# A chunked-attention and feed-forward kernel: a second seven-product scheme, also for part of the first layer, and a small addition moved to GpSimd

## The chip, the cores and the metric

The kernel runs on one core of one Trainium2 chip. The metric is device microseconds (us) of one execution; the time of the kernel before is the median of three runs. A profiled execution gives, beside its own time, a trace of every instruction, whose times count from the first instruction of the span. Engines are named PE (TensorE matmul), PEld (its weight load), DVE (VectorE), ACT (ScalarE), POOL (GpSimd) and SP (SyncE).

## The reference

```python
# q, k, v: (8, 8, 576, 64), chunks of 64 rows
scores = 0.125 * q_c @ k_c^T                  # within a chunk, 64 x 64
attn = exp(scores - max) / (sum + 1e-9)       # along the last axis
x = (attn @ v_c)                              # as 4608 tokens x 512 (heads side by side)
h = x @ w_in                                  # 512 -> 2048
g = maximum(0.01 * h, h)
out = g @ w_out                               # 2048 -> 512, float32
```

## The kernel before, in words

**Tiling.** 4608 tokens are 36 units of 128 tokens (two chunks of 64 rows each). Attention is done unit by unit; its result goes, transposed and in fp16, into a ring xT of 1536 tokens. The feed-forward part goes by blocks of tokens (`BLOCKS`, line 178): four of 128, four of 256, six of 512.

**One unit of attention.** q and k come by DMA issued from POOL (fp32 in DRAM, fp16 in SBUF), are transposed on PE (units 0 to 8, q also 13 and 18) or by a DMA of SP, q is spread into a zeroed tile QZ by two copies (POOL for the later units, line 240), PE makes the scores Sp (line 494), DVE takes the maximum and subtracts it (503, 509), ACT exponentiates (535), DVE sums (542), adds 1e-9 (544), takes the reciprocal (546) and multiplies (552); the result is transposed on PE (tpe, units 0 to 8 and 19) or by SP, PE multiplies with v (xp, line 586), and ACT writes the ring (597).

**First layer.** For each block, units "A" of PE: 512 columns of PSUM, made of 8 matmuls of 256 columns (16 of 128 in the four small blocks), line 679; ACT evacuates each with the leaky function into gT (line 693).

**Second layer.** The four small blocks are multiplied plainly (oP, line 704). In the others the block's tokens, the 2048 inner columns and the 512 output columns are each halved, and the 2x2 by 2x2 product is made of seven products ("M", line 776), each 8 matmuls of 256 columns for every 128 rows. Five of the seven take a sum of two quarters of gT, made by DVE ("form", line 753), and five a sum of quarters of w_out (WF, line 731, made once). Products 3, 2 and 1 open a PSUM bank each (ma, mb, mc), and others add to the same bank once its earlier content has been read; DVE and ACT put the results together (lines 806 to 816) and SP stores them.

**What sets the order.** `Planner` (line 22) holds all tasks with an engine, assumed durations, dependencies and a position, walks through a model of time, and emits each instruction at its planned turn; every engine and queue then runs its instructions strictly in that order. The names that steer it: `LEAD`, `ATT` (how far attention runs ahead of the blocks), `A_LEAD` (by how much of a block the first layer ends before the second layer of the block before), `MARGIN`, `HOLD`, `TWEAK`. Where PE would have a gap before 24 us, `fill` (line 942) puts idle matmuls in. PSUM has six banks for all products of this kind ("mm").

Of the kernel before, what the change touches and what calls it, by code (L numbers as in the profile page):

```python
# [21 lines left out]
class Planner:  # L22
# [61 lines left out]
    def run(self):  # L84
# [8 lines left out]
        while self.can or self.landings or any(self.queues.values()):  # L93
# [55 lines left out]
def kernel(  # L149
# [22 lines left out]
    NIN = 9  # L172
    G = 2 * CH
# [6 lines left out]
    SUBS = {}  # L180
    LEAD = 3.59
# [5 lines left out]
    ATT = -0.46  # L187
# [4 lines left out]
    EXP8 = ()  # L192
    EARLY_V = 0
    HOLD = {('v', 3): 28.7, ('vb', 1, 1): 15.3, ('k', 2): 14.1, ('q', 5, 0): 31.9, ('G', 0, 2, 0): 20.9, ('vb', 0, 0): 3.7, ('cast', 'q'): 5.0, ('n', 0): 11.9, ('k', 3): 18.8, ('c', 0): 15.1, ('e', 0): 13.3, ('tq', 4): 24.6, ('G', 0, 3, 0): 28.9, ('s', 2): 15.0, ('G', 2, 2, 0): 32.7, ('q', 5, 1): 29.5}
    EARLY_Q = ("SP",)
    T_EXP8 = 0.2
    FILL = 24.0
    FILLS = 0.8
    MARGIN = 0.6
    TWEAK = {(4, 12): 0.39, (5, 5): -0.14, (0, 4): -0.39, (17, 1): -0.17, (5, 4): -0.05, (17, 5): -0.31, (32, 1): 0.26, (33, 5): -0.04, (34, 0): 0.31}  # L200
    A_LEAD = 0.23
# [12 lines left out]
    VS = sbp.tile([128, H // 2, max(EARLY_V, 2), 128], FP16, name="VS")  # L214
# [4 lines left out]
    WF = sbp.tile([128, 5, HB, HM], FP16, name="WF")  # L219
# [10 lines left out]
    copy = {"DVE": (0.40, 0.46), "ACT": (0.52, 0.62), "POOL": (0.61, 0.66)}  # L230
# [96 lines left out]
    vf = sbp.tile([128, H // 2, max(EARLY_V, 2), D], FP32, name="v_f")  # L327

    def load_early(c, m):
        def emit(eng, tag, at):  # L330
            part = slice(m * CH, (m + 1) * CH)
            (nc.sync if eng == "SP" else nc.scalar).dma_start(
                out=vf[part, :, c, :],
                in_=v[0, m * H // 2:(m + 1) * H // 2, c * CH:(c + 1) * CH, :].rearrange("h j d -> j h d"),
            )
        return emit

    def cast_early(c, m):
        def emit(eng, tag, at):
            part = slice(m * CH, (m + 1) * CH)  # L340
            either(eng, VS[part, :, c:c + 2, part], vf[part, :, c:c + 2, :])
        return emit
# [6 lines left out]
    for c in range(EARLY_V):  # L349
        for m in range(2):  # L350
            add(("early", c, m), {e: (0.42, 0.42) for e in EARLY_Q}, load_early(c, m), [("land_f", "q0")], pos=-25 + c + 0.1 * m,
                dma=("first", 0.23, 1 / 1120))
    for c in range(0, EARLY_V, 2):
        for m in range(2):
            add(("zs", c, m), {"DVE": (0.1 + 0.105 * EARLY_V, 0.13 + 0.105 * EARLY_V)}, zero_early(m), [("warm",)], pos=-28) if c == 0 else None
            add(("vs", c, m), {"DVE": (0.46, 0.48), "ACT": (0.53, 0.62)}, cast_early(c, m),
                [("early", c, m), ("early", c + 1, m)], pos=-9.5 + c / 2)
            for e in range(2):
                v_parts.setdefault(c + e, []).extend([("vs", c, m), ("zs", 0, m)])

    def add_load(what):
# [6 lines left out]
        elif kind == "v":  # L368
# [4 lines left out]
            if b >= NVB:  # L373
                users = [u for u in range(NU) for e in range(2)
                         if (2 * u + e) // NCH == b - NVB]
                deps += [("v", max(users))]
            load(("v", b, m, c0), load_v(b, m, c0, c1), deps, (c1 - c0) * 256, "row")
            for c in range(c0, c1):
                if b * NCH + c >= EARLY_V:
                    v_parts.setdefault(b * NCH + c, []).append(("landed", "v", b, m, c0))  # L380
        elif kind == "Q":
# [27 lines left out]
    def zero_vb(i, m):  # L409
        def emit(eng, tag, at):  # L410
            to = empty(i, m)
            if eng == "DVE":
                nc.vector.memset(to, 0.0)
                return
            for t in range(2):
                part = to[:, 2 * t:2 * t + 2]
                nc.scalar.activation(
                    out=part, in_=zeros[m * CH:(m + 1) * CH, 0:1].unsqueeze(2).unsqueeze(3).to_broadcast(part.shape),
                    func=AFT.Copy, bias=0.0, scale=1.0,
                )  # L420
# [13 lines left out]
    for i in range(NVB):  # L434
        for m in range(2):
            add(("vb", i, m), {"ACT": (2.1, 2.2)} if (i, m) == (0, 0) else {"DVE": (1.02, 1.05)} if i == 0 else {"DVE": (1.02, 1.05), "ACT": (2.1, 2.2)}, zero_vb(i, m), [("warm",)] if i == 0 else [("n", 0)], pos=-27 if i == 0 else -6.0)
# [36 lines left out]
    def copy_k(u):  # L473
        def emit(eng, tag, at):
            st["KT", u] = sbp.tile([128, 4, 2, CH], FP16, name="KT", tag="KT", bufs=6)
# [3 lines left out]
    def turn_dma(name, u):  # L479
        def emit(eng, tag, at):  # L480
            n = {"q": "QT", "k": "KT"}[name]
            st[n, u] = sbp.tile([128, 4, 2, CH], FP16, name=n, tag=n, bufs={"q": 4, "k": 6}[name])
# [32 lines left out]
    def negative(u):  # L515
        def emit(eng, tag, at):
            st["nm", u] = sbp.tile([128, 8], FP32, name="nm", tag="nm", bufs=2)
            nc.vector.tensor_scalar_mul(out=st["nm", u], in0=st["mx", u], scalar1=-SCL)
        return emit

    def expo8(u):
        def emit(eng, tag, at):
            st["ex", u] = sbp.tile([128, 8, CH], FP16, name="ex", tag="ex", bufs=2)
            st["z", u] = sbp.tile([128, 8], FP32, name="z", tag="z", bufs=2)
            for i in range(8):
                nc.scalar.activation(
                    out=st["ex", u][:, i, :], in_=st["S", u][:, i, :], func=AFT.Exp,
                    bias=st["nm", u][:, i:i + 1], scale=SCL, accum_out=st["z", u][:, i:i + 1],
                )
        return emit  # L530

# [6 lines left out]
    def total(u):  # L538
        def emit(eng, tag, at):
            if u not in EXP8:  # L540
                st["z", u] = sbp.tile([128, 8], FP32, name="z", tag="z", bufs=2)
                nc.vector.tensor_reduce(out=st["z", u], in_=st["ex", u], axis=AXL.X, op=ALU.add)  # L542
            ze = sbp.tile([128, 8], FP32, name="ze", tag="ze", bufs=2)
            nc.vector.tensor_scalar_add(out=ze, in0=st["z", u], scalar1=1e-9)
            st["zi", u] = sbp.tile([128, 8], FP32, name="zi", tag="zi", bufs=2)
            nc.vector.reciprocal(out=st["zi", u], in_=ze)
        return emit

    def norm(u):
        def emit(eng, tag, at):  # L550
            st["en", u] = sbp.tile([128, 8, CH], FP16, name="en", tag="en", bufs=3)
# [13 lines left out]
    def copy_e(u):  # L565
        def emit(eng, tag, at):
            st["et", u] = sbp.tile([128, 2, 2, 2, CH], FP16, name="et", tag="et", bufs=4)
# [3 lines left out]
    def turn_e_dma(u):  # L571
        def emit(eng, tag, at):
            st["et", u] = sbp.tile([128, 2, 2, 2, CH], FP16, name="et", tag="et", bufs=4)
# [26 lines left out]
    def units1(j):  # L600
        n = BLOCKS[j] // sub(j)
        return [(j, a, h) for h in range(n) for a in range(NFC * sub(j) // 512)]

    def tile_units(u):
# [3 lines left out]
        return [("A",) + x for x in units1(j) if x[2] == h]  # L608

    for u in range(NU):  # L610
        p = att
        for n, name in enumerate("qk"):
# [6 lines left out]
            else:  # L619
                before = [x for x in range(u) if x not in BY_PE["q"]] if name == "q" else list(range(u))  # L620
                deep = {"q": 4, "k": 6}[name]
# [4 lines left out]
        if u in BY_PE["k"]:  # L626
            add(("k", u), {e: copy[e] for e in ("DVE", "ACT")}, copy_k(u), [("tk", u)] + ([("s", u - 6)] if u >= 6 else []), pos=p(u, 3))
        qdep = [("tq", u)]
        for s in range(2):
            add(("q", u, s), qe, spread_q(u, s), qdep + [("s", u - 3) if u >= 3 else ("qz", u)], pos=p(u, 2 + s))  # L630
        kt = ("k", u) if u in BY_PE["k"] else ("tk", u)
        add(("s", u), {"PE": (0.233, 0.40)}, scores(u), [("q", u, 0), ("q", u, 1), kt], pos=p(u, 4), bank="Sp", frees=[("x" if u in EXP8 else "b", u)])
# [3 lines left out]
        if u in EXP8:  # L636
            add(("nm", u), {"DVE": (0.17, 0.2)}, negative(u), [("m", u)] + freed, pos=p(u, 6))
            add(("x", u), {"ACT": (8 * T_EXP8, 8 * T_EXP8 + 0.1)}, expo8(u), [("nm", u), ("exp",)] + prev, pos=p(u, 7))
        else:
            add(("b", u), dve, shift(u), [("m", u)] + freed, pos=p(u, 6))  # L640
            add(("x", u), {"ACT": (0.53, 0.64)}, expo(u), [("b", u), ("exp",)] + prev, pos=p(u, 7))
        tz = 0.41 if u in EXP8 else 1.11
        add(("z", u), {"DVE": (tz, tz + 0.03)}, total(u), [("x", u)] + prev, pos=p(u, 8))
        ne = {"DVE": (0.70, 0.74), "POOL": (1.2, 1.25)}
        add(("n", u), {e: ne[e] for e in (NORM if u >= 9 else ("DVE",))}, norm(u),
            [("z", u)] + ([("e", u - 3)] if u >= 3 else []), pos=p(u, 9))
        ready = ("n", u)
        if u in BY_PE["e"]:
            add(("e", u), {"PE": (0.223, 0.39)}, turn_e(u), [ready, ("ident",)], pos=p(u, 10), bank="ox", frees=[("c", u)])
            add(("c", u), {e: copy[e] for e in ("DVE", "ACT")}, copy_e(u), [("e", u)] + ([("v", u - 4)] if u >= 4 else []), pos=p(u, 11))  # L650
        else:
            add(("e", u), {"SP": (1.3, 1.3)}, turn_e_dma(u), [ready] + ([("v", u - 4)] if u >= 4 else []), dma=("turn", 0.9, 0.0014), pos=p(u, -5))
        vd = [("c", u) if u in BY_PE["e"] else ("e", u)]
        for e in range(2):
            vd += v_parts[2 * u + e]
            if 2 * u + e >= EARLY_V:
                vd += [("vb", (2 * u + e) // NCH % NVB, m) for m in range(2)]
# [9 lines left out]
    def gT(j):  # L667
        return GT[START[j] // 512][:, :, START[j] % 512:START[j] % 512 + BLOCKS[j]]

# [16 lines left out]
    def act1(j, a, h):  # L686
        def emit(eng, tag, at):
            tb = sub(j)
            nf = 512 // tb
            n = START[j] // 512  # L690
            if n not in GT:
# [291 lines left out]
```

## Time and profile before

| | |
|---|---|
| median of three runs | 285.53 us (284.9 to 286.17) |
| the profiled execution, its own time | 285.76 us |
| its span, first to last instruction | 284.0 us |
| granted TensorE clock | 1.000 |
| PE busy | 273.4 us, 96% of the span |
| DVE, ACT, POOL busy | 200.6, 158.3, 130.4 us |

Rows of groups read: line, engine, operation, output and inputs, shape, count, then busy time and the mean of one in ns, then the idle time of the engine just before them and what ended it. Matmuls overlap in the pipeline (a row's mean is longer than the distance between two), so PE's pace is read from the chain of waits, where a stretch of so many matmuls has a length. Rows of the timeline begin with the start and the length in us, and end in brackets with the idle time before and what ended it.

### The profile page before, as it was taken

What the parts mean: (1) busy time and instruction counts of PE and PEld (TensorE: products, weight loads), DVE (VectorE), ACT (ScalarE), POOL (GpSimd) and SP (SyncE); (2) the same over time, 40 slices, a digit from 0 to 9 for tenths busy, and PEclk for the clock granted to TensorE, in tenths of its full rate; (3) what the DMA queues carried; (4) which work ended last, traced back from release to release, by engine and by line L of the source; (5) the groups of instructions that cost most, each with busy time, mean ns of one, the idle gap of its engine ahead of it and who ended that gap; (6) DMA issues with size and microseconds to landing.
All of it is one profiled execution on the core that took longest, in us unless ns stands there. A gap on an engine that the chain in (4) does not pass through costs nothing.

```text
span 284.0 us, 7425 instructions
## 1 busy us (share of the span) xinstructions
PE 273.4 (96%) x3076; PEld 241.2 (85%) x3076; DVE 200.6 (71%) x357; ACT 158.3 (56%) x282; POOL 130.4 (46%) x162
## 2 busy tenths in 40 slices
PE   6789999999999999999999999999999999999995
PEld 5689956778889899999899999999999999888884
DVE  6677848969897869779767987595759671810472
ACT  6279825774557476676566456545565564345320
POOL 8848655767964916645845693682230000000000
PEclk9999999999999999999999999999999999999999
DMA  8999999999999999999999999999924110400043
GB/s 142 154 190 169 176 180 155 215 134 174 146 167 174 176 161 133 185 146 158 178 130 161 151 144 196 154 128 196 155 58 166 21 32 9 150 0 2 0 168 130
DMA packets 164194, 38.77 MB, mean 137 GB/s; under 512 B 155200, under 2 KB 159808, under 8 KB 164160
## 3 DMA queue, kind: packets, MB, share of 16 engines
q0 software_dynamic: 114336, 18.09, 94.9%
q1 hardware_dynamic: 48784, 19.93, 42.1%
q8 instruction: 24, 0.39, 0.6%
q10 hardware_dynamic: 1040, 0.26, 0.5%
q14 instruction: 10, 0.08, 0.2%
HBM read 36.70 MB, written 9.44 MB: 162 GB/s over the span
## 4 chain that ended last, share of the span: by engine, by line
PE 81%; DMA 9%; POOL 7%; ACT 1%; issue 1%; DVE 0%; POOLq 0%
PE hT L679 39%; PE mb L776 13%; DMA k_in<-in_k_dram 9%; PE mc L776 9%; PE ma L776 9%; PE oP L704 4%; PE xp L586 3%; PE Sp L494 3%; POOL QZ L240 2%; POOL q_in L277 2%; POOL VB L285 1%; POOL k_in L277 1%; POOL w_inT L294 1%; ACT gT L693 1%; PE tpe L561 0%
## 5 line engine op out<-in xcount | busy, mean ns | idle before, releaser
L679 PE MATMUL hT<-xT,w_inT 128*128 128x256 f16 (+1 forms) x1280 | 141.8, 262 | 0.1
L693 ACT ACTIVATE gT<-hT 128x512 f16<-128x512 f32 x144 | 85.1, 597 | 69.8 <-PE hT L679 65.9
L679 PEld LDWEIGHTS <-w_inT 128*128 128x128 f16 x1280 | 113.3, 98 | 11.8 <-issue 0.3
L240 POOL COPY QZ<-QT 64x512 f16<-64x512 f16 x50 | 39.0, 780 | 34.9 <-DMA QT<-q_in 20.7
L776 PEld LDWEIGHTS <-gT 128*128 128x128 f16 x512 | 49.2, 98 | 5.5
L753 DVE TENSOR_TENSOR S<-gT 128x2048 f16<-128x2048 f16 (+1 forms) x30 | 30.8, 1055 | 15.8 <-ACT gT L693 15.8
L776 PEld LDWEIGHTS <-S 128*128 128x128 f16 x384 | 36.6, 98 | 4.2 <-issue 0.2
L277 POOL DMA_DIRECT2D q_in<-in_q_dram x39 | 33.2, 853 | 11.1 <-DMA q_in<-in_q_dram 5.4
L277 POOL DMA_DIRECT2D k_in<-in_k_dram x39 | 33.1, 849 | 10.4 <-DMA k_in<-in_k_dram 3.4
L542 DVE TENSOR_REDUCE z<-ex 128x8 f32<-128x512 f16 x36 | 24.5, 680 | 16.3 <-ACT ex L535 16.1
L776 PE MATMUL mb<-WF,gT 128*128 128x256 f16 x256 | 33.2, 273 | 0.0
L503 DVE TENSOR_REDUCE mx<-Sp 128x8 f32<-128x512 f32 x36 | 24.2, 672 | 7.6 <-PE Sp L494 7.5
L285 POOL DMA_DIRECT2D VB<-in_v_dram x16 | 18.5, 1159 | 21.5 <-PE xp L586 15.4
L597 ACT ACTIVATE xT<-xp 128x512 f16<-128x512 f32 x36 | 21.3, 593 | 10.3 <-PE xp L586 10.2
L552 DVE TENSOR_TENSOR en<-ex,zi 128x512 f16<-128x512 f16 x36 | 25.1, 697 | 0.4
L509 DVE TENSOR_TENSOR sh<-Sp,mx 128x512 f32<-128x512 f32 x36 | 24.6, 684 | 0.4
L535 ACT ACTIVATE ex<-sh 128x512 f16<-128x512 f32 x36 | 22.5, 626 | 3.3 <-DVE sh L509 2.8
L753 DVE TENSOR_TENSOR gT<-gT 128x2048 f16<-128x2048 f16 (+1 forms) x20 | 20.3, 1025 | 0.0
L236 ACT ACTIVATE QZ<-qp 64x512 f16<-64x512 f16 x14 | 8.2, 589 | 15.4 <-PE qp L462 9.6
L776 PE MATMUL ma<-w_outT,S 128*128 128x256 f16 x128 | 16.6, 273 | 0.1
L776 PE MATMUL mc<-WF,S 128*128 128x256 f16 x128 | 16.6, 273 | 0.0
L776 PE MATMUL ma<-WF,gT 128*128 128x256 f16 x128 | 16.6, 273 | 0.0
(53 smaller groups left out, 251.4 us busy)
## 6 DMA issues: line engine op xcount, KB each, us to landing
out_dram<-osb SPq DMA_DIRECT2D x10, 512.0 KB, 3.7
VB<-in_v_dram POOLq DMA_DIRECT2D x16, 288.0 KB, 10.6
q_in<-in_q_dram POOLq DMA_DIRECT2D x31, 128.0 KB, 11.5
k_in<-in_k_dram POOLq DMA_DIRECT2D x31, 128.0 KB, 10.7
out_dram<-osb SPq DMA_DIRECT2D x14, 256.0 KB, 6.8
w_inT<-in_moe_w_in_dram POOLq DMA_DIRECT2D x8, 256.0 KB, 7.7
w_outT<-in_moe_w_out_dram POOLq DMA_DIRECT2D x4, 512.0 KB, 11.1
q_in<-in_q_dram POOLq DMA_DIRECT2D x8, 64.0 KB, 11.6
```

The costliest lines, as they stand in the source:

```text
L240: nc.gpsimd.tensor_copy(out=out, in_=in_)
L277: nc.gpsimd.dma_start(out=qk[name, u][a - u * G:z - u * G], in_=SRC[name][a // S, :, a % S:a % S + z - a, :].rearrange("h p d -> p h d"),)
L285: nc.gpsimd.dma_start(out=VB[b % NVB][m * CH:(m + 1) * CH, :, c0:c1, m * CH:(m + 1) * CH], in_=v[b, m * H // 2:(m + 1) * H // 2, c0 * CH:c ...
L503: nc.vector.tensor_reduce(out=st["mx", u], in_=st["S", u], axis=AXL.X, op=ALU.max)
L509: nc.vector.tensor_tensor(out=st["sh", u], in0=st["S", u], in1=st["mx", u].unsqueeze(2).to_broadcast((128, 8, CH)), op=ALU.subtract,)
L535: nc.scalar.activation(out=st["ex", u], in_=st["sh", u], func=AFT.Exp, bias=0.0, scale=SCL)
L542: nc.vector.tensor_reduce(out=st["z", u], in_=st["ex", u], axis=AXL.X, op=ALU.add)
L552: (nc.vector if eng == "DVE" else nc.gpsimd).tensor_tensor(out=st["en", u], in0=st["ex", u], in1=st["zi", u].unsqueeze(2).to_broadcast((12 ...
L679: nc.tensor.matmul(out=hT[:, i, :], lhsT=w_inT[:, t, fc * 128:(fc + 1) * 128], rhs=xT[:, t, r0 % RING:r0 % RING + tb], start=(t == 0), sto ...
L693: nc.scalar.activation(out=gT(j)[:, nf * a:nf * a + nf, h * tb:h * tb + tb], in_=HT.pop((j, a, h)), func=AFT.Prelu, bias=0.0, scale=1.0, a ...
L753: nc.vector.tensor_tensor(out=to, in0=of, in1=by, op=op)
L776: nc.tensor.matmul(out=to, lhsT=lhs[:, fc, p * 128:(p + 1) * 128], rhs=rhs[:, fc, :], start=(opens and (p == 0 or j == LAST) and fc == 0), ...
```

## The change

**Second layer.** The seven products are now these (A is gT, B is w_out, both in quarters): 1 = A11 B11, 2 = A12 B21, 4 = A22 T4, 5 = S5 B12', 6 = S6 T2, 7 = S7 T3, 3 = S3 B22. There are four sums of gT instead of five, two of them made from an earlier one, and four of w_out instead of five, one written over B12 itself. ACT reads out products 1 and 2, DVE five sums as before. The products' order is 1, 6, 5, 7, 2, 4, 3; product 2 adds to the bank of 1, products 7 and 4 to that of 6, product 3 to that of 5. A product waits only for the quarters of gT that it reads.

```diff
+        (WF[:, 0], B22, B12, ALU.subtract), (WF[:, 1], WF[:, 0], B11, ALU.add), (WF[:, 2], B21, WF[:, 1], ALU.subtract),
+        (B12, B12, B11, ALU.subtract),
...
+                5: lambda: (a21, a22, ALU.add, None), 6: lambda: (SF[j, 5], a11, ALU.subtract, None),
+                7: lambda: (a11, a21, ALU.subtract, a21), 3: lambda: (a12, SF[j, 6], ALU.subtract, None),
...
-    ORDER = (3, 2, 1, 5, 4, 6, 7)
+    ORDER = (1, 6, 5, 7, 2, 4, 3)
...
+            5: qs[21] + qs[22] + before(5) + after(6), 6: [("form", j, 5)] + qs[11] + before(6) + after(3), 7: [("form", j, 5)] + qs[11],
+            3: [("form", j, 6)] + qs[12] + before(3),
```

**First layer of the last three blocks.** `L1S` names six pairs (block, k): one in block 11, two in block 12, three in block 13. A pair is four groups of 128 inner columns (two in each half) for the block's 512 tokens, and is made by the same scheme: sums of w_in (`w_form`, tile wq, once for each k) and of xT (`x_form`, tile xf, once for each block), seven products of four matmuls of 256 columns (`product1`), one read-out by ACT, five sums by DVE and four evacuations by ACT into gT (`finish1`). What is left of blocks 11 and 12 is made with matmuls of 512 columns (`SUBS`).

```diff
+    SUBS = {11:512,12:512}
+    L1S = {11:(0,),12:(0,1),13:(0,1,2)}
...
+    def product1(j, k, m):
+        def emit(eng, tag, at):
...
+            for i in range(2):
+                for t in range(2):
+                    nc.tensor.matmul(
+                        out=to[:, i, :], lhsT=lhs[:, t, i * 128:(i + 1) * 128], rhs=rhs[:, t, :],
+                        start=(m in OPENS and i == 0 and t == 0), stop=(t == 1), skip_group_check=True,
+                    )
...
+            if step == 0:
+                nc.scalar.activation(out=temp1("d", j, k), in_=of, func=AFT.Copy, bias=0.0, scale=1.0)
+            elif step == 1:
+                to, by = {6: ("w", "d"), 7: ("t", "d"), 4: ("d", "d"), 5: ("t", "t"), 3: ("w", "w")}[m]
+                nc.vector.tensor_tensor(out=temp1(to, j, k), in0=of, in1=temp1(by, j, k), op=ALU.add)
+            else:
+                make_gT(j)
...
+                deps += {2: [("lv", j, k, 1)], 7: [("lc", j, k, 6)], 4: [("lc", j, k, 7)], 3: [("lc", j, k, 5)]}.get(m, [])
```

**The 1e-9.** For units 4 to 35 the line that summed, added and inverted on DVE is three tasks: the sum on DVE, the addition on POOL (`guard`), the reciprocal on DVE.

```diff
+    ZE = range(4,99)
...
+        if u in ZE:
+            add(("zr", u), dve, total(u), [("x", u)] + prev, pos=p(u, 8))
+            add(("ze", u), {"POOL": (0.25, 0.30)}, guard(u), [("zr", u)], pos=p(u, 8))
+            add(("z", u), {"DVE": (0.21, 0.24)}, inverse(u), [("ze", u)], pos=p(u, 8))
```

**The order.** The planner's constants are changed, and so the order on every engine; the zeroing of VB is cut into eight pieces instead of four.

```diff
-    LEAD = 3.59
+    LEAD = 3.7
-    ATT = -0.46
+    ATT = -0.65
-    MARGIN = 0.6
+    MARGIN = 0.29
-    A_LEAD = 0.23
+    A_LEAD = 0.32
-    copy = {"DVE": (0.40, 0.46), "ACT": (0.52, 0.62), "POOL": (0.61, 0.66)}
+    copy = {"DVE": (0.40, 0.46), "ACT": (0.52, 0.62), "POOL": (0.66, 0.70)}
...
+                if kind == "sw" and not self.flight[True]:
+                    delay = 2.2
```

`HOLD` and `TWEAK` have other entries; the order of the loads (`LOADS`) is the same.

More of the change, by code (lines that the diff above doesn't have):

```diff
@@ L347, in zero_early @@
         return emit
-    for c in range(EARLY_V):
+    if EARLY_V:
         for m in range(2):
[L351 to L359, printed above, removed]
+            add(("zs", m), {"DVE": (0.1 + 0.105 * EARLY_V, 0.13 + 0.105 * EARLY_V)}, zero_early(m), [("warm",)], pos=-28)
     def add_load(what):
@@ L375, in add_load @@
                          if (2 * u + e) // NCH == b - NVB]
-                deps += [("v", max(users))]
+                deps += [("v", u) for u in sorted(set(users))]
             load(("v", b, m, c0), load_v(b, m, c0, c1), deps, (c1 - c0) * 256, "row")
@@ L380, in add_load @@
                     v_parts.setdefault(b * NCH + c, []).append(("landed", "v", b, m, c0))
+        elif kind == "e":
+            for m in range(2):
+                load(("e", int(rest), m), load_early(int(rest), m), [], 256, "row")
+                v_parts.setdefault(int(rest), []).extend([("landed", "e", int(rest), m), ("zs", m)])
         elif kind == "Q":
@@ L601, in units1 @@
         n = BLOCKS[j] // sub(j)
-        return [(j, a, h) for h in range(n) for a in range(NFC * sub(j) // 512)]
+        nf = 512 // sub(j)
+        return [
+            (j, a, h) for h in range(n) for a in range(NFC // nf) if nf * a % HB // 2 not in L1S.get(j, ())
+        ]
     def tile_units(u):
@@ L898 @@
                 pp = p if last else None
-                deps = list(done)
+                deps = [g for r in reads.get(m, ()) for g in qs[r]]
                 if m in SF_FORMS:
```

360 lines of the change are left out of this document (226 added, 134 removed).

## The prediction

> **What bounds the kernel now.** I read the page first (the span, each engine's busy share, the chain that ended last by engine).
>
> ```profile
> span 284.0 us, 7425 instructions
> PE 273.4 (96%) x3076; PEld 241.2 (85%) x3076; DVE 200.6 (71%) x357; ACT 158.3 (56%) x282; POOL 130.4 (46%) x162
> PE 81%; DMA 9%; POOL 7%; ACT 1%; issue 1%; DVE 0%; POOLq 0%
> ```
>
> PE is busy 96% of the span and makes 81% of the chain. A share is an average, so next I read the stretches from the first matmul of the first layer (18.30) to the last product. Columns: stretch, length, then busy time of PE, PEld, DVE, ACT, POOL with their instruction counts, the granted clock, the DMA share, GB/s.
>
> ```profile
> 18.30:60.00 41.70, 41.21 (x551) 32.59 (x552) 31.49 (x60) 29.65 (x53) 26.76 (x32) 1.00 1.86 178
> 60.00:100.00 40.00, 38.64 (x419) 34.44 (x417) 32.98 (x66) 22.37 (x43) 29.51 (x35) 1.00 1.90 162
> 100.00:187.00 87.00, 87.00 (x974) 78.70 (x972) 68.03 (x119) 52.91 (x96) 50.31 (x62) 1.00 1.82 157
> 187.00:240.00 53.00, 53.00 (x576) 47.87 (x574) 35.32 (x60) 30.91 (x54) 10.14 (x12) 1.00 0.78 97
> 240.00:280.60 40.60, 40.59 (x372) 36.13 (x370) 19.45 (x26) 13.85 (x26) 0.00 (x0) 1.00 0.19 69
> ```
>
> After 100 us PE has no gap at all, at full clock: a matmul less there is time less, provided nobody else becomes late. From 18.30 to 100 PE lacks 0.49 + 1.36 = 1.85 us, where attention only just keeps up. Ends of the span and the pace, from the chain of waits and the timeline:
>
> ```profile
> 11.07 10.43 DMA k_in<-in_k_dram
> ...
> 31.37 2.68 PE hT L679 x48
> 36.30 3.45 PE oP L704 x16
> ...
> 95.85 2.62 PE hT L679 x24
> ```
>
> ```profile
> 17.14 0.39 PE L586 MATMUL xp<-et,VB 128*128 128x64 f16 x8 [0.65 <-DMA VB<-in_v_dram]
> ...
> 18.30 1.05 PE L679 MATMUL hT<-xT,w_inT 128*128 128x128 f16 x16
> ...
> 280.63 0.42 DVE L816 TENSOR_TENSOR osb<-mb,tt 128x256 f32<-128x256 f32 x1 [0.45 <-PE mb L776]
> ```
>
> The head waits for loads (k to about 21.5, v to 17.14). The tail is one 0.42 us addition and a store. The change leaves the order of the first loads and the last block's ending pattern, so I cost both at nothing; what hides the VB zeroing's smaller pieces is this same wait for v. Pace: 24 matmuls of 256 columns take 2.62 us, 109.2 ns each; 16 of 512 columns take 3.45, 215.6 each; 48 of 128 columns take 2.68, 55.8 each.
>
> **The change part by part: PE.**
>
> ```profile
> L679 PE MATMUL hT<-xT,w_inT 128*128 128x256 f16 x1024 | 125.7, 273 | 0.0
> ```
>
> A group of 128 inner columns for 512 tokens is 4 x 2 = 8 matmuls of 256 columns; a pair is four groups, 32. By seven products of four it is 28. Six pairs: 6 x 32 = 192 become 168, 24 fewer, 24 x 109.2 = 2.62 us. `SUBS` turns the rest of blocks 11 and 12, 5 x 4 groups x 8 = 160 matmuls of 256 columns, into 80 of 512: 80 x (2 x 109.2 - 215.6) = 0.22 us. 1024 - 192 - 160 = 672 remain. The second layer has seven products before and after, with the same matmuls. The fill puts in 8 more idle matmuls, five of them after 18.30; 5 x 55.8 = 0.28 us is the most they cost. I take 0, since they stand ahead of a k that lands at about 21.5 anyway. PE's sum: -2.62 - 0.22 = **-2.84 us**.
>
> A rule of the Trainium skill speaks for more (TensorE: Matmul & The Clock Gate, "Back-to-back issue gap"): about 131 ns for a sustained 512-column matmul. As an estimate, the 80 would then save 80 x (218 - 131) = 7 us. The 215.6 ns of this trace disagree, and I go by the trace.
>
> **DVE.**
>
> ```profile
> L753 DVE TENSOR_TENSOR S<-gT 128x2048 f16<-128x2048 f16 x18 | 21.3, 1216 | 13.8 <-ACT gT L693 13.8
> L753 DVE TENSOR_TENSOR gT<-gT 128x1024 f16<-128x1024 f16 x8 | 5.4, 690 | 0.0
> ...
> L544 DVE TENSOR_SCALAR ze<-z 128x8 f32<-128x8 f32 x36 | 8.8, 245 | 1.2
> L731 DVE TENSOR_TENSOR WF<-w_outT 128x2048 f16<-128x2048 f16 x5 | 6.0, 1206 | 0.0
> L810 DVE TENSOR_TENSOR tw<-mc,td 128x512 f32<-128x512 f32 x5 | 3.5, 692 | 8.5 <-PE mc L776 8.5
> ```
>
> Removed: one sum of gT in each of ten blocks, 6 x 1.216 + 4 x 0.690 = 10.1; one of w_out, 1.2; 32 additions of 1e-9, 32 x 0.245 = 7.8. Together 19.1. Added: 24 sums wq and xf of 128x512, each about 0.690 - (1.216 - 0.690)/2 = 0.43, so 10.3; five sums in six pairs, 30 x 0.692 = 20.8. Net +12.0 us. The xf and the pairs' sums, 12 x 0.43 + 20.8 = 26 us, come after 187, where DVE is idle (53.00 - 35.32) + (40.60 - 19.45) = 38.8 us. The twelve wq, 5.2 us, stand between 20 and 36 us, in a stretch where DVE idles 41.70 - 31.49 = 10.2. Both fit, so their price is nothing as long as none comes late; without that cover it is their own time. ACT trades read-outs of products for others and stays near 56%.
>
> Where lateness could reach PE is inside a pair: products 7, 4 and 3 write to a bank that DVE must first have read. The narrowest place is the third pair of block 13: between the end of product 6 and product 7 PE has 16 matmuls, 1.75 us, and DVE has its 0.69 sum to make, perhaps behind two others: 3 x 0.69 = 2.1. The bounds for six pairs are 0 and, were each product 7 late by one sum, 6 x 0.69 = 4.1 us. I take +0.3: one late by 2.1 - 1.75, since in the trace after 100 us no wait for a bank reached PE in the second layer, which reads banks in the same way.
>
> **GpSimd's addition.**
>
> ```profile
> L277 POOL DMA_DIRECT2D q_in<-in_q_dram x39 | 33.2, 853 | 11.1 <-DMA q_in<-in_q_dram 5.4 <-DMA VB<-in_v_dram 3.3 <-DMA w_outT<-in_moe_w_out_dram 1.4
> ...
> masks.py:199 POOL TENSOR_SCALAR_AFFINE_SELECT ident<-ident 128x128 f16<-128x128 f16 x1 | 0.3, 287 | 0.1
> ...
> L967 POOL MEMSET const-uint8-127<- 128x1 uint8 x1 | 0.1, 100 | 0.0
> ```
>
> No row shows a 128x8 addition on POOL. A 128x1 memset takes 0.10, a 128x128 select 0.29; 128x8 is nearer the first, so I take 0.2 with 0.1 and 0.3 as bounds: 32 x 0.2 = 6.4 us of an engine that is 46% busy. What counts is its place: DVE's reciprocal now waits for POOL, and some 18 of the 32 additions stand directly behind a DMA issue of 0.85 us, which itself may wait for an earlier transfer. Queued behind the reciprocal are the next unit's maximum and sum, the multiplication, then PE's transpose. Today's rows of the worst case, unit 7:
>
> ```profile
> 51.78 0.68 DVE L542 TENSOR_REDUCE z<-ex 128x8 f32<-128x512 f16 x1
> 52.49 0.92 DVE L544 TENSOR_SCALAR ze<-z 128x8 f32<-128x8 f32 x1
> ```
>
> ```profile
> 52.25 2.31 POOL L285 DMA_DIRECT2D VB<-in_v_dram  x2
> 55.52 1.47 POOL L277 DMA_DIRECT2D q_in<-in_q_dram  x2 [0.96 <-DMA q_in<-in_q_dram]
> ```
>
> ```profile
> 53.74 1.91 PE L679 MATMUL hT<-xT,w_inT 128*128 128x256 f16 x16
> ```
>
> The changed order puts unit 7's addition on POOL behind the two VB and the two q_in issues, which end at 56.99. Then: addition 0.2, reciprocal 0.2, unit 8's sum 0.68, multiplication 0.70, so 58.8. PE gets to the transpose of unit 7 after four more matmuls of the small blocks (0.86), 40 of 256 columns (4.37) and one xp (0.2), counted from 53.74: 59.2. It fits by 0.4; one landing later (as the 0.96 above) it would miss by 0.6. I take 0; bounds 0 and 1.7 (two issues of 0.85 late).
>
> In the trace of before the same addition lasts 0.92 when it starts under POOL's VB issue and ends with it. The skill (SBUF — State Buffer, "Who interferes with whom") says that the port which the two engines share is locked for a whole instruction, and that a DVE operation with two SBUF inputs contends with POOL. By it each addition could wait for one 0.43 us sum, at most 32 x 0.43 = 14 us more of POOL's time. These rows agree that the two disturb each other:
>
> ```profile
> 62.86 3.34 POOL L240 COPY QZ<-QT 64x512 f16<-64x512 f16 x4
> ...
> 90.24 0.61 POOL L240 COPY QZ<-QT 64x512 f16<-64x512 f16 x1
> ```
>
> **The scores of unit 9.**
>
> ```profile
> 62.88 2.17 DVE L753 TENSOR_TENSOR S<-gT 128x1024 f16<-128x1024 f16 x2
> ```
>
> ```profile
> 64.57 0.41 PE L494 MATMUL Sp<-KT,QZ 128*128 128x64 f16 x8 [1.02 <-POOL QZ L240]
> ```
>
> PE's largest gap (1.02) waits for POOL's copies, each 0.84 beside DVE's sums against 0.61 alone. The changed order has eight more 256-column matmuls ahead of these scores (0.87), while the copies hang on the same transfers; against it stand additions on POOL ahead of the copies, up to three at 0.2. The gain is between 0 and 0.9; I take -0.3, the 0.87 less three additions, rounded.
>
> **The sum.** -2.84 (PE) - 0.3 (scores of unit 9) + 0.3 (banks of the pairs) + 0 (GpSimd's addition, DVE, ACT, head, tail) = -2.84 us. The profiled execution took 285.76 (span 284.0 and 1.76 around it): 282.92. It is 0.23 above the median of 285.53, so the forecast is 285.53 - 2.84 = **282.7 us**.
>
> **The rivals.**
>
> *The new order also closes PE's gaps* between 18 and 100 us: 1.85 more, 285.53 - 2.84 - 1.85 = 280.8. For it speaks that attention runs further ahead (`ATT`, `A_LEAD`). Against it, the loads set these gaps and their order is the same.
>
> *The banks of the pairs decide.* Half of the bound: three of six products 7 wait 0.69 each, 2.1 us, giving 285.53 - 2.84 + 2.1 = 284.8, about as before. For it, the cover of 1.75 us against up to 2.1 of DVE; against it, DVE's 38.8 us of idle time there.
>
> *POOL's queue makes it slower.* The reciprocal waits for an addition behind a DMA issue of 0.85; if that comes through to PE for the six units 7 to 12, whose attention only just keeps up, it costs 6 x 0.85 = 5.1: 285.53 - 2.84 + 5.1 = 287.8. It decides from 2.84/0.85 = 3.3 such waits on. For it: the issues wait on transfers, and the margin at unit 7 is 0.4. Against it: the chain of today has DVE at 0%, and after 100 us attention is ahead of PE.
>
> *The change does not do what it says*, if PE's pace on `product1` is worse than 109.2 because of its weight loads (PEld is busy 85%): each matmul has its own load of 128 columns, as now, so I give it no chance of its own.
>
> **How the numbers follow.** Forecast 0.60, gaps closed 0.08, banks 0.17, POOL's queue 0.15. The forecast's own range is 281.6 (scores of unit 9 gain all 0.9, nothing lost: -3.7) to 284.0 (all 1.7 at unit 7 lost, less what the scores give). The whole range goes from 281.3, a little into closed gaps, to 285.3, past the banks' case; POOL's queue and the deeper part of the closed gaps stay outside, 2 in 10. A measurement of this kernel tells 0.5% (1.43 us) from no change: under 284.1 is faster, over 286.96 slower. Faster: 0.60 + 0.08 + 0.02 of the banks = 0.70; within: 0.15 of the banks + 0.02 of the queue = 0.17; slower: 0.13.
>
> **What would show it.** Right: PE from about 18.3 to 277.8 with no gap after 100 us, 672 matmuls of 256 columns in the first layer, waits of PE before 100 us of 1.5 us or less in sum, the additions on POOL 0.1 to 0.3 each. Wrong: waits of DVE's reciprocal on POOL that are followed by waits of PE for the transposes or scores of units 7 to 12 (queue); waits of PE at la, lb or lc of `product1` on DVE's sums after 187 us (banks); 512-column matmuls away from 215.6; a first-layer start later than 18.3. If a price on POOL beyond 0.3 us shows, my bounds were too narrow.

## The result and the profile after

| | before | changed |
|---|---|---|
| median of 20 runs of each on one chip | 286.0 us (284.71 to 290.43) | 283.56 us (281.22 to 286.03) |
| ratio to the kernel before | | 0.9907 (0.9877 to 0.9936) |
| the profiled execution, its span | 285.76, 284.0 us | 283.46, 281.7 us |

0.93% faster, 2.66 us of 286.0; forecast were 2.84 us, and 282.7 us for the time. In the profiled executions it is 285.76 - 283.46 = 2.30 us. Executions of one kernel differ by some 5 us, so small differences are told by ratios with their intervals only.

The page of the changed kernel, span, busy shares and the chain by engine:

```profile
span 281.7 us, 7289 instructions
...
PE 271.9 (97%) x2980; PEld 232.8 (83%) x2980; DVE 215.0 (76%) x371; ACT 155.0 (55%) x276; POOL 138.7 (49%) x194
...
PE 87%; DVE 5%; DMA 3%; issue 2%; ACT 1%; POOL 1%; POOLq 0%
```

The stretches, as before (length, then busy PE, PEld, DVE, ACT, POOL, clock, DMA share, GB/s); the last ends a little before the last product:

```profile
18.30:60.00 41.70, 41.44 (x557) 32.93 (x554) 33.61 (x67) 27.40 (x51) 28.83 (x37) 1.00 1.88 182
60.00:100.00 40.00, 39.89 (x446) 35.85 (x445) 30.85 (x58) 22.63 (x43) 27.67 (x37) 1.00 1.85 158
100.00:187.00 87.00, 85.49 (x952) 77.10 (x951) 64.86 (x102) 51.10 (x91) 56.87 (x80) 1.00 1.88 158
187.00:240.00 53.00, 53.00 (x498) 40.21 (x496) 43.62 (x75) 29.78 (x53) 10.99 (x19) 1.00 0.75 104
240.00:277.80 37.80, 37.80 (x349) 33.88 (x347) 28.24 (x41) 14.78 (x27) 0.00 (x0) 1.00 0.15 54
```

PE is still the engine without gaps, with two differences: what it lacked before 100 us is nearly gone in this execution (0.26 + 0.11 us, against 1.85), and 1.51 us are lacking between 100 and 187, where nothing was. DVE does 17.1 us more after 187 us (43.62 + 28.24 against 35.32 + 19.45; the 26 us of added sums were costed there, the removed work was not placed), and PE does not wait for it. Three rows of PE's timeline show where its wait sits now, and where its first layer starts:

```profile
19.07 1.05 PE L677 MATMUL hT<-xT,w_inT 128*128 128x128 f16 x16
...
64.54 0.40 PE L487 MATMUL Sp<-KT,QZ 128*128 128x64 f16 x8
...
185.44 0.41 PE L575 MATMUL xp<-et,VB 128*128 128x64 f16 x8 [1.51 <-DMA et<-en]
```

The scores of unit 9 (64.54) do not wait here; an xp, unit 26's, waits for its transposed attention; and the first layer starts 0.77 us later. PE's pace in the chain of waits, the groups by form, and the last DVE addition in the timeline:

```profile
120.76 2.62 PE hT L677 x24
...
191.98 2.59 PE hT L677 x12
```

```profile
L677 PE MATMUL hT<-xT,w_inT 128*128 128x256 f16 x672 | 81.2, 273 | 0.0
...
L677 PE MATMUL hT<-xT,w_inT 128*128 128x512 f16 x80 | 19.7, 379 | 0.0
...
L523 POOL TENSOR_SCALAR ze<-z 128x8 f32<-128x8 f32 x32 | 9.7, 303 | 54.9 <-DVE z L517 54.2
...
L881 PE MATMUL la<-xT,w_inT 128*128 128x256 f16 x48 | 7.2, 273 | 0.0
...
L904 DVE TENSOR_TENSOR lt<-lb,ld 128x512 f32<-128x512 f32 x6 | 4.2, 692 | 3.6 <-PE lb L881 3.5
...
L844 DVE TENSOR_TENSOR wq<-w_inT 128x512 f16<-128x512 f16 x6 | 2.3, 412 | 0.0
```

```profile
278.27 0.42 DVE L810 TENSOR_TENSOR osb<-mc,tw 128x256 f32<-128x256 f32 x1 [0.45 <-PE mc L775]
```

From the first first-layer matmul to that addition it was 280.63 - 18.30 = 262.33 us and is 278.27 - 19.07 = 259.20: 3.13 less. PE's work accounts for -2.84 and, for five more idle matmuls of 55.8 ns, +0.28; PE's visible waits in it are 1.86 before and about 1.76 now, -0.10; the -0.47 left over is in no wait that the trace shows, and its cause is open. Against the 3.13 stand the later start, 0.77, and 0.06 of the tail: 2.30.

### The profile page after: what moved, and what is told of

It reads as the page before. It is cut to its first block, busy times and chain, and to the rows that moved or that the text cites. A ratio compares the mean times of both kernels' runs of the same rounds, so it can differ in the third digit from the quotient of the medians.

```text
span 281.7 us, 7289 instructions
## 1 busy us (share of the span) xinstructions
PE 271.9 (97%) x2980; PEld 232.8 (83%) x2980; DVE 215.0 (76%) x371; ACT 155.0 (55%) x276; POOL 138.7 (49%) x194
## 4 chain that ended last, share of the span: by engine, by line
PE 87%; DVE 5%; DMA 3%; issue 2%; ACT 1%; POOL 1%; POOLq 0%
PE hT L677 35%; PE mb L775 14%; PE mc L775 9%; PE ma L775 9%; PE oP L700 5%; DMA et<-en 3%; PE xp L575 3%; PE lb L881 3%; PE Sp L487 3%; PE la L881 2%; PE lc L881 2%; PE idle L1092 1%; PE qp L455 1%; PE tpe L550 1%; DVE VB L407 1%
## 5 line engine op out<-in xcount | busy, mean ns | idle before, releaser
L677 PE MATMUL hT<-xT,w_inT 128*128 128x256 f16 (+2 forms) x1008 | 116.9, 267 | 0.2
L677 PEld LDWEIGHTS <-w_inT 128*128 128x128 f16 x1008 | 86.4, 98 | 13.9 <-issue 0.5
L689 ACT ACTIVATE gT<-hT 128x512 f16<-128x512 f32 x120 | 70.7, 596 | 48.9 <-PE hT L677 48.1
L245 POOL COPY QZ<-QT 64x512 f16<-64x512 f16 x50 | 35.8, 716 | 17.4 <-DMA QT<-q_in 14.1
L523 POOL TENSOR_SCALAR ze<-z 128x8 f32<-128x8 f32 x32 | 9.7, 303 | 54.9 <-DVE z L517 54.2
L775 PE MATMUL mc<-w_outT,S 128*128 128x256 f16 x256 | 33.2, 273 | 0.0
L775 PE MATMUL ma<-w_outT,gT 128*128 128x256 f16 x256 | 33.2, 273 | 0.0
L775 PE MATMUL mb<-WF,S 128*128 128x256 f16 x128 | 16.6, 273 | 0.1
L575 PEld LDWEIGHTS <-VB 128*128 128x128 f16 x288 | 13.0, 98 | 3.3 <-DMA et<-en 1.8
L575 PE MATMUL xp<-et,VB 128*128 128x64 f16 x288 | 14.3, 193 | 1.5 <-DMA et<-en 1.5
```

The source lines that it names most:

```text
L245: nc.gpsimd.tensor_copy(out=out, in_=in_)
L575: nc.tensor.matmul(out=xp[:, t, e, :], lhsT=VB[b % NVB][:, t, c, :] if 2 * u + e >= EARLY_V else VS[:, t, c, :], rhs=et[:, t // 2, e, t % ...
L677: nc.tensor.matmul(out=hT[:, i, :], lhsT=w_inT[:, t, fc * 128:(fc + 1) * 128], rhs=xT[:, t, r0 % RING:r0 % RING + tb], start=(t == 0), sto ...
L689: nc.scalar.activation(out=gT(j)[:, nf * a:nf * a + nf, h * tb:h * tb + tb], in_=HT.pop((j, a, h)), func=AFT.Prelu, bias=0.0, scale=1.0, a ...
L775: nc.tensor.matmul(out=to, lhsT=lhs[:, fc, p * 128:(p + 1) * 128], rhs=rhs[:, fc, :], start=(opens and (p == 0 or j == LAST) and fc == 0), ...
```

## The experiments

All ratios are to the kernel before, run on the same chip as the edit; not all edits ran on one chip. Where the text says that the order is kept, the kernel plans as the changed one does and every other instruction keeps its engine and its place; elsewhere the planner made a new order.

| edit of the changed kernel | order | ratio (interval) |
|---|---|---|
| none | | 0.9907 (0.9877 to 0.9936) |
| none, again | kept | 0.9882 (0.9844 to 0.9920) |
| six pairs undone | new | 0.9975 (0.9944 to 1.0005) |
| nine pairs | new | 1.0195 (1.0138 to 1.0251) |
| twelve pairs | new | 1.0363 (1.0300 to 1.0426) |
| 1e-9 added on DVE | new | 0.9981 (0.9942 to 1.0020) |
| 1e-9 added on DVE | kept | 0.9922 (0.9880 to 0.9965) |
| 1e-9 not added | kept | 0.9899 (0.9860 to 0.9937) |
| VB zeroed in four pieces | new | 1.0005 (0.9971 to 1.0039) |
| ten idle matmuls, not 21 | kept | 0.9871 (0.9815 to 0.9926) |
| transposes first on SP | kept | 0.9853 (0.9796 to 0.9911) |
| both of these | kept | 0.9861 (0.9806 to 0.9915) |
| unit 9's q by PE | new | 0.9872 (0.9815 to 0.9928) |

### The changed kernel again

> The changed kernel itself, for a second profile beside the others on one chip. Theory (what the order sets comes back, what a landing sets does not): first-layer start again near 19.07 us, PE's waits before 100 us again under 1 us in sum, because the order of the instructions is the same; the one wait of 1.5 us of an xp for a transposed attention tile at 184 us is a late landing (9.3 us from issue) and may be gone. Rival (the 1.5 us wait is part of the new order): it stands again at the same unit with 1 us or more. Time 0.991 of the kernel before.

The start came at 19.52 and PE waited nowhere between 20 and 100 us. The wait at 184 us came with 0.5 us, and a second of 0.5 at 205 us, at unit 29. The place and size of the late wait go with what lands when. The late start came back, but not because of the order alone: the kernel without pairs (next section) has the same head, instruction for instruction on PE and DVE up to there, and starts the first layer at 18.34. What differs is the pace of 21 idle matmuls, first here in the changed kernel, then without pairs (a row is some 0.2 us longer than the work, since matmuls overlap):

```profile
9.00 2.43 PE L1092 MATMUL idle<-ones 128*128 128x128 f16 x21
```

```profile
9.32 1.38 PE L1092 MATMUL idle<-ones 128*128 128x128 f16 x21
...
18.34 1.05 PE L677 MATMUL hT<-xT,w_inT 128*128 128x128 f16 x16
```

### The pairs: none, nine, twelve

```diff
-    SUBS = {11:512,12:512}
-    L1S = {11:(0,),12:(0,1),13:(0,1,2)}
+    SUBS = {}
+    L1S = {}
```

> The six pairs of the first layer undone, and the 512-column matmuls with them; the four-sum scheme, the addition on GpSimd and the new constants stay. Theory (the gain is PE's saved matmuls): 24 x 109.2 + 80 x 2.8 ns = 2.84 us come back, so the time is that of the kernel before, 0.998 to 1.004. Rival (the gain is the closed gaps of the new order, the pairs give back on DVE what PE saves): it stays near 0.991.

0.9975 against 0.9907: the intervals do not overlap. The difference, 0.0068 of 286.0, is 1.9 us; the intervals' ends allow 0.2 to 3.7, so 2.84 fits. Against the changed kernel's second ratio, of the same chip (0.9882), it is 0.0093, 2.7 us. What is left of the change without the pairs, 0.25%, cannot be told from nothing. The ratio alone does not show that it was the pairs: this edit came with a new order, and the three new orders below that keep six pairs came out at 0.9872, 0.9981 and 1.0005. The traces speak for the pairs. The pages show (here without pairs) that PE's busy time is 2.6 us more and DVE's 27.3 less, and no wait takes their place between 100 and 187 us.

```profile
span 282.0 us, 7425 instructions
...
PE 274.5 (97%) x3084; PEld 243.0 (86%) x3084; DVE 187.7 (67%) x319; ACT 151.7 (54%) x268; POOL 138.2 (49%) x194
```

```profile
100.00:187.00 87.00, 87.00 (x972) 78.63 (x971) 65.62 (x104) 50.73 (x91) 58.45 (x81) 1.00 1.85 156
```

From the first first-layer matmul to the last addition PE is busy 260.45 us before, 260.08 without pairs, and 257.42 and 257.58 in the changed kernel's two profiles. So 2.5 to 2.7 us of PE's work went with the pairs.

This profiled execution (283.77 us, where the median is 285.38) is only 0.3 us longer than the changed kernel's, since it starts the first layer at 18.34 and has no late wait: a single profile would have shown the pairs to be worth nothing.

```diff
-    L1S = {11:(0,),12:(0,1),13:(0,1,2)}
+    L1S = {11:(0,1,2),12:(0,1,2),13:(0,1,2)}
```

> Nine pairs instead of six (three in each of blocks 11, 12, 13), order planned for it. PE has 12 matmuls of 256 columns less and 12 of 512 less: each pair saves (32 - 28) x 109.2 = 0.44 us, some 1.3 us for three. Theory (after about 205 us PE alone sets the end, and DVE, idle 8.6 of the last 60 to 19 of the last 91 us, covers 3 x 5 x 0.69 = 10.4 us more): 0.4 to 0.6% below the changed kernel, 0.984 to 0.987 of the kernel before, no wait of PE on DVE's sums. Rival (the sums' cover is used up): waits of PE at the pairs or the second layer's sums of 1 us or more, time as with six pairs or above.

The rival, and much more of it: 2% slower than before, 0.0288 or 8.2 us above six pairs, though PE has less to do (84 matmuls of 256 columns stand in place of 48 of 512, 1.2 us less). PE's waits in the trace with nine pairs, the stretch where they lie, and the longest of them:

```profile
PE la L881 <- ACT ld L901: 3.9, 2, 3.7
...
PE Sp L487 <- DMA KT<-k_in: 1.7, 1, 1.7
...
PE xp L575 <- DMA et<-en: 0.8, 1, 0.8
PE la L881 <- DVE lw L904: 0.6, 1, 0.6
PE lc L881 <- DVE lt L904: 0.4, 1, 0.4
```

```profile
205.00:240.00 35.00, 28.40 (x274) 22.02 (x272) 30.01 (x49) 18.83 (x35) 3.36 (x8) 0.95 0.27 60
```

```profile
226.31 1.22 DVE L751 TENSOR_TENSOR S<-S,gT 128x2048 f16<-128x2048 f16 x1
...
227.44 1.22 DVE L751 TENSOR_TENSOR gT<-gT 128x2048 f16<-128x2048 f16 x1
228.58 1.22 DVE L751 TENSOR_TENSOR S<-gT,S 128x2048 f16<-128x2048 f16 x1
...
231.82 0.63 ACT L511 ACTIVATE ex<-sh 128x512 f16<-128x512 f32 x1 [1.88 <-DVE sh L502]
232.36 1.06 ACT L901 ACTIVATE ld<-la 128x512 f32<-128x512 f32 x2
...
232.99 1.23 PE L881 MATMUL la<-xT,w_inT 128*128 128x256 f16 x5 [3.68 <-ACT ld L901]
```

PE is busy 28.40 of 35 us, DVE 30.01. What holds PE is a chain through engines that run strictly in order: DVE makes three sums of the second layer, two of xT and then the maximum and difference of an attention unit; ACT's exponential waits 1.88 us for these; behind the exponential on ACT stands the pair's read-out ld; and PE's next product needs the bank that it reads. DVE need not be full over the stretch for that (86%), it needs only to be next in line with something else. The wait also costs more than its length: behind it PE's granted clock is 0.60 between 233 and 237 us, with 23 matmuls in these 4 us, against 45 in the next 4 at 1.00. That is some 2 us more, an estimate from the 22 matmuls that are missing.

> Twelve pairs, three more in block 10, whose first layer runs where attention still does (before 190 us). Theory: PE saves 2.6 us against six pairs, but DVE gets 20.8 us more, more than the 18.9 us that it idles after 187 in the changed kernel, so sums come late: no better than nine pairs, 0.985 to 0.995 of the kernel before, with PE's waits on DVE's sums in the trace. Rival (DVE's load still fits): 0.980 to 0.984.

Worse than both expected: 1.0363. Here DVE itself is nearly full between 187 and 240 us, in an execution of 301.18 us; PE waits there 3.5 us for ACT's read-out ld again, and 3.3 us in seven waits for DVE:

```profile
187.00:240.00 53.00, 43.41 (x435) 33.92 (x433) 50.77 (x84) 28.96 (x52) 13.15 (x21) 0.97 0.84 105
```

### The addition of 1e-9

> The addition of 1e-9 back on DVE for all units. Theory (its place costs and gives nothing that reaches PE): 0.988 to 0.994 of the kernel before, DVE's reciprocal waits for POOL (5.7 us in the changed kernel) gone, without effect on the end. Rival A (GpSimd's addition delays attention): faster than the changed kernel, down to 0.985. Rival B (DVE needs the 8 to 9 us that the additions take): slower, 0.996 or more, with PE's waits for xp or scores before 190 us.

```diff
-    ZE = range(4,99)
+    ZE = ()
```

0.9981, what rival B gave. But the planner had ordered everything anew, and the main waits in its profile (two of an xp, together 2.5 us, after 180 us) name a transfer; only 0.3 us at 150 us name DVE. That does not say whether DVE made the transfer late. So the same edit in the kept order:

```diff
-            (nc.vector if eng == "DVE" else nc.gpsimd).tensor_scalar_add(out=st["ze", u], in0=st["z", u], scalar1=1e-9)
+            nc.vector.tensor_scalar_add(out=st["ze", u], in0=st["z", u], scalar1=1e-9)
```

> The 32 additions of 1e-9 run on DVE at the places that they have now; every other instruction keeps its engine and its place (unlike x2, where the planner made a new order; it gave 0.998 of the kernel before). Theory A (x2's loss is DVE's 32 x 0.29 us = 9.4 us more on a chain that paces attention until 205 us): 0.994 to 1.000, with PE's waits for attention (xp, scores, tpe) summing to 2 us more than the 1.0 to 1.5 us of the changed kernel. Theory B (x2's loss came with its new order, the addition itself is free on either engine): 0.986 to 0.992, DVE's 5.7 us of waits on POOL gone.

0.9922, between the two, with an interval that holds both the changed kernel's and theory A's lower end. Whether DVE's additions cost up to half a percent stays open. What can be settled is the other side, by leaving the addition out:

```diff
-            st["ze", u] = sbp.tile([128, 8], FP32, name="ze", tag="ze", bufs=2)
-            (nc.vector if eng == "DVE" else nc.gpsimd).tensor_scalar_add(out=st["ze", u], in0=st["z", u], scalar1=1e-9)
+            st["ze", u] = st["z", u]
```

> The addition of 1e-9 is left out for all 36 units (the reciprocal is taken of the sum itself); every other instruction keeps its engine and its place. It bounds what the addition can cost where it stands. Theory (on GpSimd it costs nothing that reaches PE): 0.986 to 0.992 of the kernel before, as the changed kernel. Rival (DVE's wait of 5.7 us in all for GpSimd's result delays attention): 0.984 or below, and PE's waits for xp and scores between 60 and 205 us under 0.5 us.

0.9899, as with it. On GpSimd the addition gives no delay that can be measured, so the larger loss of the first run is either DVE's time or its new order; the same edit in the kept order, nearer to the changed kernel, speaks for the order, without showing it. In this execution PE waited 2.1 us at unit 9's scores, so leaving the addition out did not close that gap.

### The head

> The zeroing of VB in four pieces and with the due times of the kernel before (the first piece on ACT, the last two after the first unit's multiplication). Theory (the changed head is late by DVE's work: pieces of 0.54 us stand ahead of the cast of the first q, which begins at 5.54 instead of 4.74 though q is there at 4.63): the first-layer start goes from 19.07 back to 18.0 to 18.5 us and the time falls by 0.6 to 0.9 us, to 0.988 to 0.989 of the kernel before. Rival (loads set the head): start and time stay.

```diff
...
-            for t in range(2):
-                add(("vb", i, m, t), {"DVE": (0.53, 0.56), "ACT": (1.05, 1.15)}, zero_vb(i, m, t), [("warm",)], pos=ZPOS + i)
+            add(("vb", i, m), {"ACT": (2.1, 2.2)} if (i, m) == (0, 0) else {"DVE": (1.02, 1.05)} if i == 0 else {"DVE": (1.02, 1.05), "ACT": (2.1, 2.2)}, zero_vb(i, m), [("warm",)] if i == 0 else [("n", 0)], pos=-27 if i == 0 else -6.0)
...
```

The start came forward to 18.05, as the theory said, and the time did not follow: 1.0005, worse by a percent than the changed kernel. Again a new order; its profile has waits of 0.5 us at 51, 0.4 at 148 and 1.5 at 154 us. What the changed head does is read in its chain of waits:

```profile
3.08 0.54 DVE VB L407
3.78 0.54 DVE VB L407
4.39 0.54 DVE VB L407
5.54 0.86 DVE q_in L243
...
9.19 2.25 PE idle L1092 x21
```

DVE zeroes VB while q is already there, so the first q is cast at 5.54 and not at 4.74; then 21 idle matmuls at 107 ns keep the second unit waiting until 11.44. The second is undone alone, in the kept order:

```diff
...
+        n = 10 if 7.0 < since < 8.0 else n
...
```

> Ten idle matmuls in place of 21 between the first unit's scores and the second unit's q, all else in the same order. Theory (in the changed head 21 idle matmuls at 107 ns, not 56, stand in the way: 9.19 to 11.44, while the q that they stand before landed at 9.38): the second q's transposes come 0.8 to 1.2 us earlier and the first layer starts at 18.0 to 18.6 instead of 19.07 or 19.52; if PE's work sets the end, the time falls by as much, to 0.984 to 0.988 of the kernel before. Rival (transfers set the pace until about 205 us): the start is earlier, but the waits of xp for the transposed attention after 180 us grow by the same and the time stays at 0.988 to 0.991.

The first layer starts at 18.42. The ratio, 0.9871, is in the theory's range, and its interval (0.9815 to 0.9926) holds the rival's range and the changed kernel's ratio as well, so the run does not decide. The timeline with ten idle matmuls shows where the earlier start ends in this execution:

```profile
18.42 1.05 PE L678 MATMUL hT<-xT,w_inT 128*128 128x128 f16 x16
...
65.13 0.41 PE L488 MATMUL Sp<-KT,QZ 128*128 128x64 f16 x8 [1.15 <-POOL QZ L246]
```

PE starts 0.65 us earlier and here waits 1.15 us for GpSimd's copies. (The execution, 282.04 us, is still 1.4 us shorter than the changed kernel's, mainly because no xp waits at 184 us.) In the profiles of the changed kernel (two), of this one and of two more in the kept order below and above, unit 9's scores began at 64.5 to 66.8 us, whenever the first layer began: 64.54 after a start at 19.07, 65.13 after 18.42. From the start to these scores it is 45.5 us in each of the five, less the wait there (0, 0, 1.15, 1.87, 2.06): an earlier start gains only where the copies come early too.

### The late transposes

```diff
+    move(("e", 26), ("n", 26))
+    move(("e", 27), ("n", 27))
+    move(("tq", 31), ("e", 27))
```

(`move(a, b)` puts the instruction of task a directly behind that of b.)

> On SP's queue the transposes of units 26 and 27's attention go ahead of the transposes of k 30 and q 31, all else in the same order. Theory (the 1.5 us wait at 184 us is SP's order: the multiplication of unit 26 ended at 171.35, but its transpose was issued at 176.09, behind q's and k's of unit 30): issue near 172, landing near 181 to 183, the wait of that xp at 184 gone; 0.7 to 1.5 us less, 0.983 to 0.988 of the kernel before. Rival (the transfers' rate sets it): the landing moves less than 1 us, or the wait comes back at a unit behind (28 to 30, the wait at 204 us of the second profile) and the time stays.

SP's queue in the changed kernel, and what its chain of waits says:

```profile
171.52 1.97 SPq L476 DMA_TRANSPOSE QT<-q_in  x1
173.58 2.40 SPq L476 DMA_TRANSPOSE KT<-k_in  x1
176.09 2.29 SPq L563 DMA_TRANSPOSE et<-en  x1
```

```profile
176.09 9.31 DMA et<-en
...
185.44 0.41 PE xp L575 x8
```

With the move the wait at this xp is gone; that execution waited 1.9 us at unit 9's scores, 100 us ahead of the moved instructions. 0.9853 is the lowest ratio of all and in the theory's range, but its interval holds the changed kernel's ratio. Both edits together:

> Ten idle matmuls and the transposes first, together. Theory (PE's work sets the end, both losses are on its path): the sum of both gains, 1.5 to 2.5 us below the changed kernel, 0.979 to 0.985 of the kernel before. Rival (transfers set the pace until 205 us): not below the better of the two alone.

0.9861: not below the better of the two, as the rival said; the sum of both gains would have been 0.979 to 0.985, which the interval (0.9806 to 0.9915) does not rule out. Whether either edit gains stays open.

### Unit 9's q by PE

```diff
-    BY_PE = {'q': (0, 1, 2, 3, 4, 5, 6, 7, 8, 13, 18), 'k': (0, 1, 2, 3, 4, 5, 6, 7, 8), 'e': (0, 1, 2, 3, 4, 5, 6, 7, 8, 19)}
+    BY_PE = {'q': (0, 1, 2, 3, 4, 5, 6, 7, 8, 9, 13, 18), 'k': (0, 1, 2, 3, 4, 5, 6, 7, 8), 'e': (0, 1, 2, 3, 4, 5, 6, 7, 8, 19)}
```

> Unit 9's q is transposed by PE and spread by DVE or ACT, so the scores of unit 9 no longer wait for SP's transpose and GpSimd's copies; PE gets 4 transposes (0.22 us) more; order planned for it. In six profiles of one order those scores began at 64.5 to 67.4 us, with PE's wait there 0 to 3.1 us, whenever the first layer began. Theory (the landings of the loads before 64 us set that point): the wait moves to unit 10's scores or to a tpe or xp nearby and the time stays within 0.987 to 0.994. Rival (only SP's and GpSimd's steps of that one unit are late): no wait of PE between 60 and 75 us, 0.980 to 0.986.

The wait moved on by one unit, as the theory said:

```profile
70.17 0.41 PE L487 MATMUL Sp<-KT,QZ 128*128 128x64 f16 x8 [1.60 <-POOL QZ L245]
```

No version here is told apart from the changed kernel as faster.

## Why the prediction was right

**PE's sum: right.** 672 matmuls of 256 columns and 80 of 512 stand in the trace, 24 in 2.62 us and 12 in 2.59, and the pairs' products form no gap. Without the pairs 2.5 to 2.7 us of PE's work are back and the gain is gone but for 0.25%. That the time came within 0.2 us of the forecast is in part luck, since the other terms of the profiled execution (start, gaps, late wait, the -0.47 left over) cancel. The trace stood against the 131 ns of the Trainium skill (TensorE: Matmul & The Clock Gate, "Back-to-back issue gap"): 2.59 / 12 = 215.8 ns, so the estimate of 7 us did not come.

**DVE: right, a little more than costed.** The sums wq took 0.412 (0.43 estimated), the pairs' sums 0.684 to 0.692; DVE's busy time rose by 14.4 us, not 12.0. With six pairs PE never waited for one of them. The +0.3 for the banks was not there.

**The rival of the banks: right in kind, wrong in its place.** It does not decide at six pairs; nine cost 8.2 us more than six, where I had bounded six by 4.1. Products do wait for a bank to be read, but the longest waits are for ACT's read-out of product 1 (3.9 us in two waits), and only 1.5 us in four are for DVE's sums, the reader that I had in mind. I had looked at block 13's third pair for its cover of 1.75 us; it broke in blocks 11 and 12, whose pairs share DVE and ACT with the last units of attention.

**GpSimd's addition: right at nothing, with two errors that cancel.** Unit 7 in the changed kernel, GpSimd, DVE and PE:

```profile
55.11 1.38 POOL L282 DMA_DIRECT2D q_in<-in_q_dram  x2
56.56 0.78 POOL L523 TENSOR_SCALAR ze<-z 128x8 f32<-128x8 f32 x1
57.37 0.20 DVE L529 RECIPROCAL zi<-ze 128x8 f32<-128x8 f32 x1
...
57.60 0.69 DVE L517 TENSOR_REDUCE z<-ex 128x8 f32<-128x512 f16 x1
58.20 0.68 DVE L541 TENSOR_TENSOR en<-ex,zi 128x512 f16<-128x512 f16 x1
...
59.49 0.39 PE L550 MATMUL tpe<-ident,en 128*128 128x128 f16 x4
```

58.8 was worked out for the multiplication's end and 59.2 for PE; they came at 58.88 and 59.49. That agreement is luck in part: GpSimd's issues ended at 56.49, 0.50 earlier than taken, and the addition lasted 0.58 longer. The price was mis-sized: 0.303 us on average, not 0.2, and beyond the 0.3 that I had as its bound; a median of 0.23 with six of 0.50 to 0.78. Each of the six begins beside a DVE operation that reads two tiles in SBUF (the one at 56.56 a sum of w_out from 56.03 to 57.25) and ends 0.09 to 0.10 us after it; so does a seventh, which began late in such a sum and took 0.27. The additions that begin beside a DVE operation reading PSUM (at 113.84, 138.45 or 148.56, for example) take 0.23. That is what the Trainium skill's lock (SBUF — State Buffer, "Who interferes with whom") says, and the trace agrees; but it struck 7 of 32, not all, far from the 14 us estimated from it. POOL's queue as the rival that makes it slower fell with the kernel without the addition.

**The head at nothing: wrong in the profiled execution, by 0.77 us.** I had named the wait for v as the cover. v's second half landed at 15.6 and covered nothing. DVE's zeroing makes the first q late, but the kernel without pairs has the same zeroing and starts at 18.34: the 0.77 us are the idle matmuls at half pace. Nor did PE wait for the k that I expected at about 21.5: its transposes came at 22.52 with no wait ahead of them, so the added idle matmuls stood in the way of work. Whether the later start costs the median anything is not shown: with ten idle matmuls unit 9's scores waited instead in the one profile, and the ratio does not decide.

**The closed gaps: held to be unlikely (0.08), and half true.** PE's waits before 100 us did fall from 1.85 to 0.37 us in this execution; in three others with this order of attention, 1.15 to 2.06 us stand at unit 9 again. The time did not follow, since a start later by 0.77 and a wait of 1.51 us at 184 us stand against it. My -0.3 and +0.3 were right only in that they cancel, which is luck: a gain of 1.02 at unit 9's scores and losses at places that I had not named.

## What to carry to other kernels

Where one engine has no gaps, counting its instructions at the pace read from the chain gives the gain; terms that lie under another bound (here waits for transfers, seen until about 205 us) can be large and cancel. A scheme that trades matmuls for sums pays only where the engines that read its banks have nothing else queued: six pairs gained, and three more in blocks 11 and 12 lost, with DVE 86% busy. Test an edit in the order that stands, since an edit that came with a new order (the zeroing) took back the whole gain though its own effect, the earlier start, was there.

## What had not been expected of the hardware

**Idle matmuls at half pace.** Idle matmuls ahead of real work can delay it. Early in the changed kernel 21 matmuls of 128 columns took 2.25 us, 107 ns each, later ones 55.8 ns. In that execution the granted clock showed 0.50 there; in the second profile of the same kernel the clock showed 1.00 throughout, and the same 21 took the same time. The Trainium skill (TensorE: Matmul & The Clock Gate, "Wait — 56ns, not 53.3ns?") gives 106.7 ns for a cold and 55.6 ns for a warm array at this size; the trace agrees, and the granted clock of the profile does not always show it. The same 21 ran at the full pace in the profile without pairs, so with one and the same head the pace can differ.

**Landings differ from one execution to the next.** With all of PE's, DVE's and GpSimd's work up to there in one order, unit 9's scores began at 64.54 in one profile and at 66.81 in another (the one with the late transposes moved, 100 us behind). In the two profiles without a wait there, PE waited at 184 us instead (1.5 and 0.5 us); in the three with one it did not, though in one of these the transposes had been moved.
